# First layernorm of a two-layer attention and MLP kernel: x halves on two DMA queues, root on ScalarE, quarter copies, and Q of the first tiles in banks of its own

## Chip, cores, metric

The kernel runs on one core of one Trainium2 chip. The metric is device microseconds of one execution; lower is better. PE is TensorE, PEld its weight load, DVE VectorE, ACT ScalarE, POOL GpSimd, SP SyncE.

## The reference, cut to what matters

```python
x = A_x                                             # 2048 x 1024, bf16
x = x + A(_layernorm(x), A_wqkv, A_wo)              # sliding, dilated attention, 32 heads
x = x + B(_layernorm(x), B_w1, B_b1, B_w2, B_b2)    # MLP with GELU, 3584 wide
# ... the same two lines once more
# _layernorm: (x - mean) / sqrt(var + 1e-5) along the row, no scale, no shift
```

The change touches only the first layernorm (rows 0 to 511, "tiles" 0 to 3 of 128 rows) and the Q projection behind it.

## The kernel before

A row tile of x is loaded, its mean and variance are taken on VectorE, the inverse root on GpSimd; VectorE normalises, TensorE transposes 128x128 blocks into PSUM, ScalarE copies them to SBUF. Then the projections start. Tiles 0 and 1 go first, in 256-column matmuls over six chunks of Q; tiles 2 and 3 follow into the other half of the same PSUM banks.

```python
load_x(0, 0, 2)                              # x tiles 0 and 1 whole, SyncE's queue
load_wq_piece(wq_first[0], 0)                # Q weights in four pieces of 512 KB
load_x(0, 2, 4)
for k in range(2, KD, 2):
    load_wq_piece(wq_first[k // (KD // 2)], k)
# ...
def ln_stats(t, mv=None, rstd=None):         # ... bn_stats x2, bn_aggr on VectorE, then
    pool.tensor_tensor(out=rstd[:], in0=mv[:, 1:2], in1=eps_t[:], op=ALU.add)
    pool.tensor_tensor(out=rstd[:], in0=rstd[:], in1=mhalf[:], op=ALU.pow)
# ... in gen_qkv, for the first group of rows:
for kq in range(4 if n == 0 else 0):
    for c in range(6):
        first[c] = qkv_chunk(wq, c, xnT, first.get(c), kq * 2, (kq + 1) * 2, 0, 2)
        if (kq, c) in ((1, 5), (2, 5)):
            transpose_on_pe(*first_late.pop(0))        # tiles 2 and 3
for c in range(NCH):
    ps = qkv_chunk(wq, c, xnT, first[c], t0=2) if c in first else qkv_chunk(wq, c, xnT)
    act.copy(qT[:, c, :], ps[:])
```

A small helper keeps an engine's instructions in program order where it is switched on; elsewhere a scheduler orders them when the kernel is built.

## Time and profile before

| before | value |
|---|---|
| time, median of the six runs beside the changed kernel | 1232.80 us (1232.70 to 1232.99) |
| PE busy | 1226.2 of 1231.0 us |
| first projection matmul starts | 9.53 us |
| first copy of K starts | 26.39 us |
| end of the last addition to x, end of the span | 1228.40, 1230.96 us |

From the page of the kernel before, the busy times of the engines and the chain of work that ended last:

```profile
PE 1226.2 (100%) x5777; PEld 631.8 (51%) x5777; DVE 869.1 (71%) x886; ACT 304.1 (25%) x475; POOL 126.4 (10%) x238
...
PE 99%; DVE 0%; DMA 0%; ACT 0%; POOL 0%; issue 0%
```

PE is busy nearly all the time and makes up nearly the whole chain (99%). "Busy" alone would not say that PE is the limit, since its ends are modelled; the waits do. The view of waits of the kernel before, matmuls only (who waited for whom, us in total, times, longest us):

```profile
PE acc L118 <- DVE big L93: 1.1, 1, 1.1
PE acc L118 <- ACT xnT L93: 0.6, 1, 0.6
```

In 1231 us the view lists two waits of PE, both in the first 10 us (it leaves out idle time of 0.15 us or less). This is how the head runs; the timeline gives start, duration, engine, what is written and read, and in brackets how long the engine had been idle and what ended that:

```profile
0.80 1.28 ACT L93 ACT_TABLE_LOAD   x1 [0.80 <-PEq L592]
...
3.54 1.28 DVE L93 BATCH_NORM_STATS2 stats<-x 128x6 f32<-128x512 bf16 x2 [2.54 <-DMA x<-in_A_x_dram]
...
6.38 0.49 DVE L93 TENSOR_SCALAR xn<-x,mv,rstd 128x1024 bf16<-128x1024 bf16 x1
...
7.00 0.56 POOL L93 TENSOR_TENSOR rstd<-rstd,mhalf 128x1 f32<-128x1 f32 x1
...
7.59 0.55 DVE L93 TENSOR_SCALAR xn<-x,mv,rstd 128x1024 bf16<-128x1024 bf16 x1 [0.72 <-POOL rstd L93]
...
8.25 0.61 PE L211 MATMUL acc<-ident,xn 128*128 128x128 bf16 x8
...
8.89 1.07 ACT L93 COPY xnT<-acc 128x512 bf16<-128x512 bf16 x2 [0.24 <-PE acc L211]
...
9.53 2.78 PE L118 MATMUL acc<-xnT,wt 128*128 128x256 bf16 x24 [0.56 <-ACT xnT L93]
```

The activation table is loaded at 0.80 us, when ScalarE has nothing to do. Norm 0 (the normalising of tile 0) follows the statistics of tile 1 at once; norm 1 waits 0.72 us for GpSimd's power. ScalarE's half copy takes about 0.6 us and releases the first projection matmul at 9.53 us. The transposes of tiles 2 and 3 then stand between matmuls, and the view shows no wait for them. (The starts show a small one: tile 3's transposes begin at 14.00 us, 0.20 us after the matmul before instead of 0.11, when ScalarE's copy of tile 2 is done at 13.96.) The first copy of K is a good mark for the end of the head, as PE is unbroken behind it:

```profile
26.39 0.59 ACT L93 CAST kT<-acc 128x512 bf16<-128x512 f32 x1 [1.14 <-PE acc L118]
```

### The profile page before, as it was taken

Reading aid. Unit: us, or ns where it says so; the run is one execution under the profiler, and the core shown is the slowest. Engines: PE = TensorE matmul, PEld = TensorE weight load, DVE = VectorE, ACT = ScalarE, POOL = GpSimd, SP = SyncE. Lnnn points to the kernel's source line nnn. Section 1 sums busy time; section 2 is a strip of 40 time slices with the busy share of each in tenths; the row PEclk is TensorE's granted clock in tenths of the full one; section 3 lists DMA queues with packets and bytes.
Section 4 is the critical chain, followed back from the end, with each engine's and each line's share of the span. In section 5 each row is a group of like instructions: output and inputs, shape, how many; then the busy total and the mean of one; then the engine's idle time right before and its main releaser. Section 6 shows DMA issues by size and latency. Waiting matters only on the chain.

```text
span 1231.0 us, 13956 instructions
## 1 busy us (share of the span) xinstructions
PE 1226.2 (100%) x5777; PEld 631.8 (51%) x5777; DVE 869.1 (71%) x886; ACT 304.1 (25%) x475; POOL 126.4 (10%) x238
## 2 busy tenths in 40 slices
PE   9999999999999999999999999999999999999999
PEld 6666544456444564445544465444654444444444
DVE  7999899995996999376992779927599698012001
ACT  4333152014310143202431024310244101400310
POOL 4010011101021102200031000210000102000000
PEclk9999999999999999999999999999999999999999
DMA  9954568647487647756476565766556668446441
GB/s 307 283 180 140 184 198 202 207 138 235 144 197 227 178 163 180 220 171 187 148 189 222 171 171 169 175 220 197 171 183 158 185 200 204 160 159 196 154 135 53
DMA packets 219359, 226.63 MB, mean 184 GB/s; under 512 B 68562, under 2 KB 187488, under 8 KB 216224
## 3 DMA queue, kind: packets, MB, share of 16 engines
q1 hardware_dynamic: 214704, 208.69, 55.3%
q0 software_dynamic: 4592, 17.05, 6.0%
q8 instruction: 45, 0.74, 0.2%
q14 instruction: 18, 0.15, 0.1%
HBM read 197.40 MB, written 6.29 MB: 165 GB/s over the span
## 4 chain that ended last, share of the span: by engine, by line
PE 99%; DVE 0%; DMA 0%; ACT 0%; POOL 0%; issue 0%
PE acc L118 99%; DMA x<-in_A_x_dram 0%; DVE stats L93 0%; PE L L118 0%; PE acc L211 0%; PE L L211 0%; ACT xnT L93 0%; DVE mv L93 0%; DVE x L93 0%; POOL rstd L93 0%
## 5 line engine op out<-in xcount | busy, mean ns | idle before, releaser
L118 PE MATMUL acc<-xnT,wt 128*128 128x512 bf16 (+1 forms) x3376 | 720.8, 376 | 0.6 <-ACT xnT L93 0.6
L118 PEld LDWEIGHTS <-wt 128*128 128x128 bf16 x3376 | 399.1, 119 | 320.1 <-issue 1.6
L118 PE MATMUL acc<-wt,hT 128*128 128x512 bf16 (+1 forms) x1820 | 388.1, 376 | 0.0
L118 PEld LDWEIGHTS <-hT 128*128 128x128 bf16 x1820 | 178.1, 98 | 209.0
L93 DVE TENSOR_TENSOR big<-big 128x2048 bf16<-128x2048 bf16 (+2 forms) x184 | 245.5, 1359 | 2.9
L93 ACT ACTIVATE hT<-acc,b1T 128x512 bf16<-128x512 f32 x224 | 152.4, 688 | 331.1 <-PE acc L118 331.0
L93 DVE TENSOR_TENSOR big<-qT,kT 128x4096 bf16<-128x4096 bf16 x64 | 143.8, 2286 | 26.7 <-ACT kT L93 26.1
L93 DVE TENSOR_TENSOR big<-abc,vT 128x4096 bf16<-128x4096 bf16 x64 | 144.8, 2286 | 24.0 <-DMA abc<-a_d 23.5
L93 DVE TENSOR_TENSOR tmp<-acc,b2bc 128x512 f32<-128x512 f32 x56 | 38.6, 690 | 148.6 <-PE acc L118 145.1
L93 ACT CAST qT<-acc 128x512 bf16<-128x512 f32 x64 | 37.2, 586 | 341.7 <-PE acc L118 341.7
L118 PE MATMUL acc<-wt,oT 128*128 128x512 bf16 x448 | 97.8, 379 | 0.0
L93 DVE BATCH_NORM_STATS2 stats<-x 128x6 f32<-128x512 bf16 x128 | 83.4, 678 | 4.0 <-DMA x<-in_A_x_dram 3.4
L118 PEld LDWEIGHTS <-oT 128*128 128x128 bf16 x448 | 43.8, 98 | 52.8
L93 DVE TENSOR_TENSOR x<-acc,big 128x512 bf16<-128x512 f32 (+1 forms) x9 | 5.7, 633 | 90.0 <-PE acc L118 90.0
L93 POOL TENSOR_TENSOR rstd<-mv,eps_t 128x1 f32<-128x1 f32 x60 | 23.5, 391 | 434.2 <-DVE mv L93 434.2
L93 ACT CAST vT<-acc 128x512 bf16<-128x512 f32 x64 | 37.5, 586 | 83.1 <-PE acc L118 83.1
L93 ACT CAST kT<-acc 128x512 bf16<-128x512 f32 x64 | 37.4, 588 | 67.3 <-PE acc L118 67.3
L93 DVE TENSOR_TENSOR x<-acc,x 128x512 bf16<-128x512 f32 x64 | 42.5, 667 | 4.9 <-PE acc L118 4.7
L93 POOL TENSOR_TENSOR rstd<-rstd,mhalf 128x1 f32<-128x1 f32 x60 | 43.8, 730 | 4.7
L93 DVE TENSOR_SCALAR xn<-x,mv,rstd 128x1024 bf16<-128x1024 bf16 x52 | 28.2, 543 | 18.4 <-POOL rstd L93 18.4
L93 POOL DMA_DIRECT2D big<-big x24 | 13.5, 568 | 256.0 <-DVE big L93 239.1
L93 DVE TENSOR_TENSOR x<-tmp,x 128x512 bf16<-128x512 f32 x56 | 38.6, 690 | 1.6
(60 smaller groups left out, 251.1 us busy)
## 6 DMA issues: line engine op xcount, KB each, us to landing
wt<-in_B_w_dram SPq DMA_DIRECT2D x56, 1024.0 KB, 6.1
wt<-in_B_w_dram SPq DMA_DIRECT2D x64, 896.0 KB, 4.8
wt<-in_A_wqkv_dram SPq DMA_DIRECT2D x46, 1024.0 KB, 5.8
wt<-in_A_wo_dram SPq DMA_DIRECT2D x16, 1024.0 KB, 5.0
abc<-a_d POOLq DMA_DIRECT2D x32, 256.0 KB, 5.1
big<-big POOLq DMA_DIRECT2D x24, 256.0 KB, 7.8
x<-in_A_x_dram SPq DMA_DIRECT2D x16, 256.0 KB, 6.0
out_dram<-x SPq DMA_DIRECT2D x31, 128.0 KB, 2.2
```

The costliest lines, as they stand in the source:

```text
L93: inst = f(*args, **kwargs)
L118: return pe(nc.tensor.matmul(*args, **kwargs))
```

## The change

Its intent: start the projections earlier. x lands in halves over two queues, the root is spread over ScalarE and VectorE, copies come in quarters so that the first matmul needs only the first quarter, and Q of tiles 0 and 1 is copied out of banks of its own, so that two more chunks keep PE busy until tile 3 is there.

```diff
-    load_x(0, 0, 2)
+    for t in range(2):
+        sp.dma_start(x[t][:, 0:HALF], x_in[t * P:(t + 1) * P, 0:HALF])
+        act.dma_start(x[t][:, HALF:], x_in[t * P:(t + 1) * P, HALF:])
-    load_wq_piece(wq_first[0], 0)
-    load_x(0, 2, 4)
-    for k in range(2, KD, 2):
+    for k in range(0, KD, 2):
         load_wq_piece(wq_first[k // (KD // 2)], k)
+        if k < 4:
+            load_x(0, 2 + k // 2, 3 + k // 2)
 ...
+            act.activation(stds[tt][:], mvs[tt][:, 1:2], ACT.Sqrt, bias=eps_t[:])   # was two GpSimd ops
+            vec.reciprocal(rstd[:], stds[tt][:])
 ...
+        transpose_on_pe(xn0, xa[0][:, 0, :, :], parts=[act.copy] * 4)
+        transpose_on_pe(xn1, xa[0][:, 1, :, :], parts=[vec.tensor_copy] * 2 + [act.copy] * 2)
+        warm_up(2)
 ...
-                if (kq, c) in ((1, 5), (2, 5)):
+                if kq == 3:
+                    act.copy(qT[:, c, 0:2 * P], first[c][:, 0:2 * P])
+                if (kq, c) in ((2, 5), (3, 5)):
                     transpose_on_pe(*first_late.pop(0))
+        for c in range(6 if n == 0 else NCH, NCH):
+            ps = qkv_chunk(wq, c, xnT, t0=0, t1=2)
+            act.copy(qT[:, c, 0:2 * P], ps[:, 0:2 * P])
 ... (tiles 2 and 3 of all chunks then in fresh banks; a generator for later layernorms, same work)
```

More of the change, by code (lines that the diff above doesn't have):

```diff
@@ L181, in transpose_bias @@
         pe(nc.tensor.transpose(ps[:], b1_rows[:], ident[:KF, :KF]))
-        act.copy(b1T[:], ps[:])
+        return ps
     def ln_stats(t, mv=None, rstd=None):
@@ L205, in ln_norm, with transpose_on_pe @@
         return xn
-    def transpose_on_pe(xn, out, pst=None, halves=1):
+    def transpose_on_pe(xn, out, pst=None, parts=None):
         if pst is None:
@@ L211, in transpose_on_pe @@
             pe(nc.tensor.transpose(pst[:, k, :], xn[:, k * P:(k + 1) * P], ident[:]))
-        n = KD // halves
-        for h in range(halves):
-            act.copy(out[:, h * n:(h + 1) * n, :], pst[:, h * n:(h + 1) * n, :])
+        parts = parts or [act.copy]
+        n = KD // len(parts)
+        for h, copy in enumerate(parts):
+            copy(out[:, h * n:(h + 1) * n, :], pst[:, h * n:(h + 1) * n, :])
     last_transpose = [None]
@@ L227, in ln_first, with stats @@
         xa[0] = new_xnT()
-        vec.on = True
+        vec.on = act.on = True
         both = psum.tile([P, 2, KD, P], BF16, name="L", bufs=1)
-        stats = {}
-        def norm(tt):
-            xn = ln_norm(tt, *stats.pop(tt))
-            if tt < 2:
-                transpose_on_pe(xn, xa[0][:, tt, :, :], halves=2)
-            else:
-                first_late.append((xn, xa[0][:, tt, :, :], both[:, tt - 2, :, :]))
-            if tt == 0:
-                warm_up(4)
-        stats[0] = ln_stats(0)
-        stats[1] = ln_stats(1)
-        norm(0)
-        norm(1)
-        transpose_bias()
-        stats[2] = ln_stats(2)
-        stats[3] = ln_stats(3)
-        norm(2)
-        norm(3)
-        vec.on = False
+        mvs = {}
+        stds = {}
+        def stats(tt):
+            st6 = lnp.tile([P, 2, 6], F32, name="stats")
+            for h in range(2):
+                vec.bn_stats(st6[:, h, :], x[tt][:, h * HALF:(h + 1) * HALF])
+            mvs[tt] = lnp.tile([P, 2], F32, name="mv")
+            vec.bn_aggr(mvs[tt][:], st6[:])
+            stds[tt] = lnp.tile([P, 1], F32, name="std")
+            act.activation(stds[tt][:], mvs[tt][:, 1:2], ACT.Sqrt, bias=eps_t[:])
+        def norm(tt):
+            rstd = lnp.tile([P, 1], F32, name="rstd")
+            vec.reciprocal(rstd[:], stds[tt][:])
+            return ln_norm(tt, mvs[tt], rstd)
+        stats(0)
+        stats(1)
+        xn0 = norm(0)
+        xn1 = norm(1)
+        transpose_on_pe(xn0, xa[0][:, 0, :, :], parts=[act.copy] * 4)
+        ps = transpose_bias()
+        transpose_on_pe(xn1, xa[0][:, 1, :, :], parts=[vec.tensor_copy] * 2 + [act.copy] * 2)
+        warm_up(2)
+        act.copy(b1T[:], ps[:])
+        stats(2)
+        stats(3)
+        for tt in range(2, 4):
+            first_late.append((norm(tt), xa[0][:, tt, :, :], both[:, tt - 2, :, :]))
+        vec.on = act.on = False
+        act.hold()
     def new_xnT(pool=None):
@@ L273, in qkv_chunk @@
             mm(ps[:, t0 * P:t1 * P], lhsT=wts[k // (KD // 2)][:, k % (KD // 2), c::NCH], rhs=xnT[:, t0:t1, k, :],
-               start=(k == 0 and t0 == 0), stop=(k == KD - 1), skip_group_check=t1 - t0 < NTT)
+               start=(k == 0), stop=(k == KD - 1), skip_group_check=t1 - t0 < NTT)
         return ps
@@ L314, in gen_qkv @@
         if n == 0:
-            ln_early(1)
+            early_tiles = ln_early((1, None), (2, qk_next))
+            for _ in range(NTT):
+                next(early_tiles)
             wv = load_qkv(2)
-            ln_early(2, qk_next)
+            for _ in early_tiles:
+                pass
             load_x(3)
@@ L323, in gen_qkv @@
                 first[c] = qkv_chunk(wq, c, xnT, first.get(c), kq * (KD // 4), (kq + 1) * (KD // 4), 0, 2)
-                if (kq, c) in ((1, 5), (2, 5)):
+                if kq == 3:
+                    act.copy(qT[:, c, 0:2 * P], first[c][:, 0:2 * P])
+                if (kq, c) in ((2, 5), (3, 5)):
                     transpose_on_pe(*first_late.pop(0))
+        for c in range(6 if n == 0 else NCH, NCH):
+            ps = qkv_chunk(wq, c, xnT, t0=0, t1=2)
+            act.copy(qT[:, c, 0:2 * P], ps[:, 0:2 * P])
         for c in range(NCH):
-            ps = qkv_chunk(wq, c, xnT, first[c], t0=2) if c in first else qkv_chunk(wq, c, xnT)
-            act.copy(qT[:, c, :], ps[:])
+            t0 = 2 if n == 0 else 0
+            ps = qkv_chunk(wq, c, xnT, t0=t0)
+            act.copy(qT[:, c, t0 * P:], ps[:, t0 * P:])
             yield
@@ L504, in ln_a, with ln_early @@
             ln_tile((n % NG) * NTT + tt, tt, xa[n], ahead=ahead)
-    def ln_early(n, pool=None):
-        xa[n] = new_xnT(pool)
-        xns = bigp.tile([P, NTT, D], BF16, name="big") if pool is None else pool.tile([P, NTT, D], BF16, name="qT")
-        vec.on = True
-        s = [ln_stats(n * NTT)]
-        for tt in range(NTT):
-            if tt + 1 < NTT:
-                s.append(ln_stats(n * NTT + tt + 1))
-            ln_norm(n * NTT + tt, *s[tt], xns[:, tt, :])
-            sp.dma_start_transpose(xa[n][:, tt, :, :], xns[:, tt, :].rearrange("s (k p) -> s k p", p=P))
-        vec.on = False
+    def ln_early(*groups):
+        tiles = []
+        for n, pool in groups:
+            xa[n] = new_xnT(pool)
+            xns = bigp.tile([P, NTT, D], BF16, name="big") if pool is None else pool.tile([P, NTT, D], BF16, name="qT")
+            tiles += [(n * NTT + tt, xns[:, tt, :], xa[n][:, tt, :, :]) for tt in range(NTT)]
+        vec.on = True
+        ahead = ln_stats(tiles[0][0])
+        for i, (t, xn, xT) in enumerate(tiles):
+            mv_rstd = ahead
+            if i + 1 < len(tiles):
+                ahead = ln_stats(tiles[i + 1][0])
+            ln_norm(t, *mv_rstd, xn)
+            sp.dma_start_transpose(xT, xn.rearrange("s (k p) -> s k p", p=P))
+            if i + 1 == len(tiles):
+                vec.on = False
+            yield
     def stage(gen, count=None, sides=()):
@@ L542 @@
     pool.on = True
-    warm_up(16)
+    warm_up(14)
     ln_first()
```

## The prediction

> **What bounds the kernel.** TensorE. The page gives PE busy 1226.2 of 1231.0 us at full clock; the chain of waits is PE, unbroken from 9.5 us to 1228.0 us. The view of waits shows two for PE matmuls: 1.1 us for the warm-up's memset, 0.6 us for ScalarE's copy before the first projection matmul. So the change can only move that first matmul (9.53 us), or open a gap after it: a few us in 1233 at most.
>
> **The head before** (timeline, 0 to 22 us): x lands 3.51; statistics of tiles 0 and 1 end 6.46; norm 0 starts 6.38; norm 1 waits 0.72 us for GpSimd, ends 8.14; eight transposes 0.61; half copy 0.59; matmul 9.53.
>
> **What the change does there.**
> - x halves on two queues: the same 512 KB must come first; at most 0.2 us. The Trainium skill ("DMA: Bandwidth & Descriptors", Issuing engines are not separate DMA queues) says queues share engines and only issue time is saved; the two x issues took 0.87 us together here.
> - Square root on ScalarE, reciprocal on VectorE for two GpSimd operations (0.38 + 0.56). But in the built order the activation-table load stands behind the wait for tile 0's aggregate, where before it ran at 0.80 us. A load costs 1.28 us in this trace, and the one at 154.7 us did wait for VectorE first. So: aggregate seen at about 4.9, load until 6.2, both roots until 6.8, norm 0 starts about 6.8 (0.4 later), norm 1 about 7.45, ending about 8.0 (0.15 earlier). The load eats most of the gain.
> - Quarter copies, tile 1's first two on VectorE: about 0.3 to 0.37 each (from 1.01 for 1024 columns, 0.59 for 512) instead of 0.59. The two new warm-up matmuls end about 9.1. First projection matmul about 9.1: gain 0.4 us.
>
> **What it gives back.**
> - Q of the first group becomes 128 matmuls of 256 columns at 0.109 us, before 96 of them and 16 of 512 at 0.216: +0.05 us.
> - In ScalarE's order six Q copies (about 0.3 each) stand between the copies of tiles 2 and 3 (1.0 each). Tile 3's ends about 17.3 us; PE wants it about 17.0: a new wait of 0 to 0.7 us, 0.3 expected.
> - One more table load before the first exponential (67 us) delays VectorE about 1 us. VectorE's attention products end 2.2 us before the output projection starts (125.3), so PE should not feel it.
>
> **Prediction:** 1232.6 us, range 1231.6 to 1233.6; faster by over 2% 0.01, within 2% 0.98, slower 0.01.
>
> **What the profile would show.** Right: table load from about 4.9 us; norm 0 near 6.8, norm 1 ending near 8.0; first projection matmul near 9.1; a PE wait for tile 3's copy at about 17 us; first K copy within 0.3 us of 26.39; no other PE wait. Wrong: first projection matmul before 8.6 or after 9.6; no wait at 17 us (gain 0.4) or one over 0.8 (a loss); a PE wait at 60 to 130 us.
>
> **What would make it wrong.** The table load hidden after all (gain near 1 us); ScalarE's queue starting late, second halves of x landing after 3.9 us; VectorE copies from PSUM over 0.5 us each, which also pushes tiles 2 and 3 back; weight pieces late behind the reordered x loads.

## The result

The changed kernel takes 1233.43 us (median of six runs, 1233.09 to 1233.62), the kernel before 1232.80 in the same rounds. The ratio is 1.0005, with a 95% interval of 0.9992 to 1.0018. A ratio here is the mean time of one kernel's runs over that of the other's of the same rounds, so it is not quite the ratio of the medians. Every one of the six runs is above every one of the six before, and the trace says where 0.6 to 0.8 us went.

Waits of PE and of its weight loads in the changed kernel, first 40 us:

```profile
PE acc L118 <- DVE big L93: 1.1, 1, 1.1
...
PE acc L213 <- DVE xn L93: 0.8, 1, 0.8
...
PEld L118 <- DMA wt<-in_A_wqkv_dram: 0.2, 1, 0.2
PE acc L118 <- ACT xnT L93: 0.2, 1, 0.2
```

The 0.8 us before the transposes is no loss in itself (two warm-up matmuls fewer stand there). The last two lines are new and lie behind the first projection matmul. The head, as the timeline shows it:

```profile
3.61 1.29 DVE L93 BATCH_NORM_STATS2 stats<-x 128x6 f32<-128x512 bf16 x2 [2.61 <-DMA x<-in_A_x_dram]
...
4.93 0.21 DVE L93 BATCH_NORM_AGGREGATE mv<-stats 128x2 f32<-128x12 f32 x1
...
5.22 1.28 ACT L93 ACT_TABLE_LOAD   x1 [5.22 <-DVE mv L93]
...
6.51 0.48 ACT L93 ACTIVATE std<-mv,eps_t 128x1 f32<-128x1 f32 x2
6.84 0.16 DVE L93 RECIPROCAL rstd<-std 128x1 f32<-128x1 f32 x1 [0.31 <-ACT std L93]
7.04 0.55 DVE L93 TENSOR_SCALAR xn<-x,mv,rstd 128x1024 bf16<-128x1024 bf16 x1
...
7.70 0.55 DVE L93 TENSOR_SCALAR xn<-x,mv,rstd 128x1024 bf16<-128x1024 bf16 x1
...
8.31 0.62 PE L213 MATMUL acc<-ident,xn 128*128 128x128 bf16 x8
...
8.97 0.49 DVE L93 COPY xnT<-acc 128x256 bf16<-128x256 bf16 x2 [0.73 <-PE acc L213]
...
9.41 4.34 PE L118 MATMUL acc<-xnT,wt 128*128 128x256 bf16 x36
...
12.22 1.30 PEld L118 LDWEIGHTS <-wt 128*128 128x128 bf16 x12 [0.23 <-DMA wt<-in_A_wqkv_dram]
```

The table load now starts at 5.22 us, released by VectorE's aggregate of tile 0 (the step that joins the statistics of its two halves), and both square roots stand behind it. VectorE's reciprocal waits 0.31 us for ScalarE. Norm 0 is 0.66 us later than before (7.04 against 6.38), norm 1 0.11 us later (7.70 against 7.59). The quarter copies then win 0.20 us: from the end of tile 1's transposes to the first projection matmul 0.47 us (8.94 to 9.41) against 0.67 (8.86 to 9.53). Tile 1's transposes end 0.08 us later, so the net gain at that matmul is 0.12 us. At 12.22 us a weight load waits for the third piece of Q weights.

The chain of waits of the changed kernel from tile 2's transposes on (start, us, what):

```profile
13.76 0.46 PE L L213 x8
...
14.24 1.01 ACT xnT L93
15.25 1.66 ACT qT L93 x6
16.91 0.93 ACT xnT L93
...
17.88 22.26 PE acc L118 x134
```

Here ScalarE has the chain for 3.6 us: tile 2's copy, six copies of Q, tile 3's copy. PE has matmuls of its own for nearly as long, and waits for the rest. The PE starts nearest to it are 17.45 and 17.88 us: 0.43 us apart where 0.11 is usual, so 0.32 us are lost. The view of waits says 0.2, because it counts from the modelled end of the last matmul.

The first copy of K:

```profile
26.79 0.58 ACT L93 CAST kT<-acc 128x512 bf16<-128x512 f32 x1 [1.35 <-PE acc L118]
```

It is 0.40 us later than before: -0.12 + 0.22 (weight piece: the two starts there are 0.27 and 0.17 us apart instead of 0.11) + 0.32 = 0.42. (The rest, about 0.02 us less, is explained under experiment 5.) This offset stays to the end, where the last addition to x ends 0.41 us later (1228.81 against 1228.40). But the span is 0.78 us longer: 0.37 us more arise after the last addition, 2.93 us in place of 2.56. No part of the change runs there.

The trace's SyncE waits for DMA semaphores after the last addition, start in us and the semaphore's number (left out are the issue of the last output DMA and one wait for semaphores outside this list, which comes ahead of it; the last output DMA is number 116 before, 100 in the changed kernel):

```
before:   1228.88 wait 101   1228.94 wait 111   1229.01 wait 112   1229.07 wait 113   1229.13 wait 114
          1229.24 wait 115   1230.00 wait 116   1230.06 wait 117   1230.12 drain ... span ends 1230.96
changed:  1230.41 wait 100   1230.47 wait 102   1230.54 wait 112   1230.60 wait 113   1230.66 wait 114
          1230.72 wait 115   1230.78 wait 116   1230.84 wait 118   1230.90 drain ... span ends 1231.74
```

A semaphore here is a counter that a DMA raises as it lands. SyncE waits for eight semaphores of its DMAs one after the other, 0.06 us each. Before, the DMA that lands last (1229.98 us) is the seventh of the eight. In the changed kernel it (1230.39 us) is the first, and seven waits that are long fulfilled follow it. The last DMA itself is no later: it lands 1.58 us after the end of the last addition in both. The built program gives its DMAs these semaphores in turn, and the changed kernel has two DMAs more, which moves the last one from the seventh place to the first. Six more waits of 0.06 us behind it are the 0.37 us. That is only a reading of one pair of traces; experiments 1, 2 and 6 test it.

### The profile page after: what moved, and what is told of

It is laid out like the page before. It is cut to its first block, busy times and chain, and to the rows that moved or that the text cites. A ratio compares the mean times of both kernels' runs of the same rounds, so it can differ in the third digit from the quotient of the medians.

```text
span 1231.7 us, 13998 instructions
## 1 busy us (share of the span) xinstructions
PE 1226.3 (100%) x5789; PEld 632.5 (51%) x5789; DVE 870.1 (71%) x892; ACT 306.4 (25%) x490; POOL 122.7 (10%) x230
## 4 chain that ended last, share of the span: by engine, by line
PE 99%; ACT 0%; DMA 0%; DVE 0%; issue 0%; ACTq 0%
PE acc L118 99%; DMA x<-in_A_x_dram 0%; ACT xnT L93 0%; ACT qT L93 0%; DVE stats L93 0%; ACT L93 0%; PE acc L213 0%; PE L L118 0%; DVE xn L93 0%; PE L L213 0%; DVE x L93 0%; ACT std L93 0%; DVE mv L93 0%; DVE rstd L93 0%; PE acc L183 0%
## 5 line engine op out<-in xcount | busy, mean ns | idle before, releaser
L93 ACT CAST qT<-acc 128x512 bf16<-128x512 f32 (+1 forms) x72 | 38.0, 545 | 341.2 <-PE acc L118 341.2
L93 DVE TENSOR_REDUCE z<-e 128x128 f32<-128x1024 f32 x8 | 15.3, 1918 | 33.7 <-ACT e L93 33.7
```

What stands on the lines that cost most here:

```text
L93: inst = f(*args, **kwargs)
```

## The experiments

Twelve runs, all with correct outputs, in three batches; the kernels of a batch share one chip and its runs of the kernel before (medians 1232.88, 1232.94 and 1232.70 us): runs 1 to 4, 5 to 8 and 9 to 12. Positions are those of one profiled execution per kernel, so small differences between batches may be the chip's. Every verdict was "same" at 2%; what follows rests on positions in the traces, and times stand beside them. Where no profile line is shown, positions and landing times of single DMAs are read from the trace.

| run | median us (runs) | before | first projection | first K copy | after the last addition |
|---|---|---|---|---|---|
| before | 1232.80 (6) | | 9.53 | 26.39 | 2.56 |
| changed | 1233.43 (6) | 1232.80 | 9.41 | 26.79 | 2.93 |
| 1 before, x1 on ACT's queue | 1233.61 (4) | 1232.88 | 10.83 | 27.60 | 2.55 |
| 2 changed, one queue | 1233.20 (4) | 1232.88 | 8.93 | 26.55 | 2.93 |
| 3 changed, early table | 1232.96 (4) | 1232.88 | 8.80 | 25.96 | 2.93 |
| 4 changed, tile 3 on DVE | 1234.24 (4) | 1232.88 | 9.26 | 27.47 | 2.92 |
| 5 changed, copy order | 1232.77 (5) | 1232.94 | 9.40 | 26.25 | 2.92 |
| 6 before, two DMAs more | 1233.06 (5) | 1232.94 | 9.53 | 26.30 | 2.93 |
| 7 combination | 1232.36 (5) | 1232.94 | 9.27 | 26.11 | 2.50 |
| 8 combination, load order | 1232.59 (5) | 1232.94 | 9.16 | 26.08 | 2.49 |
| 9 whole tiles | 1233.82 (5) | 1232.70 | 8.78 | 27.40 | 2.50 |
| 10 halves | 1233.75 (5) | 1232.70 | 8.65 | 27.61 | 2.49 |
| 11 changed, root on GpSimd | 1233.19 (5) | 1232.70 | 9.44 | 26.60 | 2.94 |
| 12 changed again | 1233.22 (5) | 1232.70 | 9.46 | 26.62 | 2.92 |

### 1. Before, tile 1 of x through ScalarE's queue

```diff
-    load_x(0, 0, 2)
+    load_x(0, 0, 1)
+    act.dma_start(x[1][:], x_in[P:2 * P, :])
```

> The kernel before, with one edit: x tile 1 is loaded through ScalarE's DMA queue. In the changed kernel 0.40 us of the 0.74 us longer span arise in the first 26 us (first K copy 26.79 against 26.39) and 0.34 us after the last addition to x (from its end to the end of the span 2.94 us against 2.56). Theory A: the end of the program takes longer because a second DMA queue is in use; then this kernel's stretch after the last addition is about 2.9 us, its first K copy stays within 0.1 us of 26.39, and it is about 0.3 us slower than before. Rival B: the 0.34 us at the end is scatter from run to run; then 2.5 to 2.6 us and no slower than before.

Theory A (a second queue costs the end) fell: a second queue is in use and the end takes 2.55 us. The expectation that the head stays was wrong too, and this is the more useful miss. Statistics of tile 0 in the head of this run:

```profile
4.84 1.29 DVE L93 BATCH_NORM_STATS2 stats<-x 128x6 f32<-128x512 bf16 x2 [3.85 <-DMA x<-in_A_x_dram]
```

Tile 0 landed at 4.82 us and tile 1 at 4.65, where the kernel before has 3.51 and 4.14 on one queue. The two transfers share the engines, so the tile that is needed first comes 1.3 us later. The first projection matmul slips to 10.83 us and the first K copy to 27.60.

### 2. The changed kernel on one queue

```diff
-        act.dma_start(x[t][:, HALF:], x_in[t * P:(t + 1) * P, HALF:])
+        sp.dma_start(x[t][:, HALF:], x_in[t * P:(t + 1) * P, HALF:])
```

> The changed kernel with all four x halves on SyncE's queue, so no second queue. Theory A: the stretch after the last addition falls to about 2.6 us and the kernel gains 0.3 us against the changed one. Rival B: no change at the end. In the head: the last half of x is issued about 0.9 us later (each issue takes 0.43 us), so if the second queue's saved issue time matters, the first projection matmul comes later than 9.41 by up to 0.5 us; if the loads of weights are bound by what the DMA engines move, the first K copy stays within 0.15 us of 26.79.

The end stays at 2.93 us without a second queue: theory A falls a second time. Rival B (scatter) falls as well, as every kernel with two DMAs more than before shows 2.92 to 2.94. The head moved the other way than feared. The halves of tile 0 landed at 3.10 and 3.41 us (3.58 and 3.76 on two queues), those of tile 1 at 4.65 and 4.93 (4.09 and 4.32):

```profile
3.13 1.29 DVE L93 BATCH_NORM_STATS2 stats<-x 128x6 f32<-128x512 bf16 x2 [2.13 <-DMA x<-in_A_x_dram]
...
8.93 2.81 PE L118 MATMUL acc<-xnT,wt 128*128 128x256 bf16 x24
...
11.99 1.53 PE L118 MATMUL acc<-xnT,wt 128*128 128x256 bf16 x12 [0.24 <-DMA wt<-in_A_wqkv_dram]
```

Statistics start 0.48 us sooner and so does the first projection matmul. Then 0.46 us of PE time go in waiting for the third weight piece at 11.99 us, and the first K copy gains only 0.24 us. The other profiles with tile 0 in halves agree: its later half lands at 3.41 to 3.50 us on one queue (four profiles) and at 3.59 to 3.83 on two (six). Against experiment 4, which has the changed kernel's head on the same chip, the first projection matmul is 0.33 us sooner (8.93 against 9.26). The second queue is no gain in this head; one queue in the order of need was better.

### 3. The table load early

```diff
     pool.memset(eps_t[:], EPS)
+    root0 = const.tile([P, 1], F32, name="root0")
+    act.activation(root0[:], eps_t[:], ACT.Sqrt)
```

> The changed kernel plus one early square root of a constant on ScalarE, so that the activation-table load runs at about 1 us instead of behind tile 0's aggregate at 5.22 us. Theory C: the load (1.28 us) costs about 0.5 us at the first projection matmul (8.9 instead of 9.41), but this is not kept: the third weight piece lands at 12.18 us and x of tile 3 at 10.91 us whatever ScalarE does, so the PE wait for the weight piece grows from 0.2 to about 0.7 us and the first K copy stays within 0.1 us of 26.79. Rival D: the load is the whole loss; then the first K copy comes at about 26.3 us and the kernel is about 0.5 us faster than the changed one.

```profile
1.73 1.28 ACT L93 ACT_TABLE_LOAD   x1 [1.73 <-PEq L623]
...
6.29 0.11 DVE L93 RECIPROCAL rstd<-std 128x1 f32<-128x1 f32 x1
...
6.43 0.55 DVE L93 TENSOR_SCALAR xn<-x,mv,rstd 128x1024 bf16<-128x1024 bf16 x1
...
7.09 0.55 DVE L93 TENSOR_SCALAR xn<-x,mv,rstd 128x1024 bf16<-128x1024 bf16 x1
...
8.80 4.12 PE L118 MATMUL acc<-xnT,wt 128*128 128x256 bf16 x36
```

The reciprocal no longer waits for ScalarE, and the first projection matmul comes at 8.80 us, 0.61 us sooner. Of this 0.17 us are an earlier landing of x (statistics at 3.44 against 3.61), so about 0.44 us are the table load. Experiment 4 is a closer control: the changed kernel's head on the same chip, with statistics from 3.46 us and the late table load, has its first projection matmul at 9.26 us, which again leaves 0.44. Theory C expected the gain to be lost again at the third weight piece; it was not, as that piece landed at 11.25 us in this run and not at 12.18. The first K copy at 25.96 us beats rival D's 26.3. The landing of weights differs between profiles of programs with the same loads, and C had taken one landing time for a constant. The time, 1232.96 us, is near that of the kernel before because the end still costs 0.37 us and tile 3 still waits.

### 4. Tile 3's copy on VectorE

```diff
-                    transpose_on_pe(*first_late.pop(0))
+                    transpose_on_pe(*first_late.pop(0), parts=[vec.tensor_copy] if kq == 3 else None)
```

> The changed kernel with tile 3's transposed copy (1024 columns) on VectorE instead of ScalarE, where it stood behind six Q copies. Theory: the PE gap before 17.88 us (about 0.3 us) goes; first K copy at about 26.48 us, span 0.3 us shorter than the changed kernel's. Rival: something else holds PE there (a later arrival of tile 3's norm or of a bank), and the gap stays over 0.2 us.

The opposite came out:

```profile
14.99 0.61 PE L213 MATMUL L<-ident,xn 128*128 128x128 bf16 x8
...
16.57 1.28 DVE L93 BATCH_NORM_STATS2 stats<-x 128x6 f32<-128x512 bf16 x2
...
17.77 0.67 DVE L93 COPY xnT<-L 128x1024 bf16<-128x1024 bf16 x1
...
18.50 1.75 PE L118 MATMUL acc<-xnT,wt 128*128 128x256 bf16 x14 [1.14 <-DVE xnT L93]
```

The transposes were done at 15.6 us and the copy itself takes 0.67 us instead of 1.0, but the scheduler put it behind the statistics of a later tile, so it started at 17.77. The PE starts around it are 17.08 and 18.50 us, a loss of 1.3 us. This experiment does not show that the place in ScalarE's queue was the cause of the first gap, only that the place in VectorE's queue decides this one.

### 5. Tile 3's copy further ahead in ScalarE's queue

```diff
-                if kq == 3:
+                if kq == 3 and c < 2:
                     act.copy(qT[:, c, 0:2 * P], first[c][:, 0:2 * P])
                 if (kq, c) in ((2, 5), (3, 5)):
                     transpose_on_pe(*first_late.pop(0))
+        for c in range(2, 6 if n == 0 else 0):
+            act.copy(qT[:, c, 0:2 * P], first[c][:, 0:2 * P])
```

The built order has four Q copies before tile 3's copy instead of six.

> The changed kernel with ScalarE's copy of tile 3 moved ahead of the last Q copies (only four of the six now stand before it). Theory: the wait before tile 3's first matmul comes from the place of that copy in ScalarE's queue (in the run with the copy on VectorE it stood behind statistics there and the gap grew to 1.4 us), so here the gap of 0.43 us between two PE starts at about 17.5 us goes to 0.11, and the first K copy comes 0.32 us sooner for the same start: 17.06 us after the first projection matmul plus any wait for weights, against 17.38 in the changed kernel. Rival: a bank or the norm of tile 3 holds PE; then the gap stays over 0.3 us. Weight pieces: their landing scattered by 1.7 us between runs of one and the same head (third piece 12.18 and 10.65 us), so a wait for them may or may not show.

```profile
PE acc L213 <- DVE xn L93: 1.8, 1, 1.8
PE acc L118 <- DVE big L93: 1.0, 1, 1.0
```

These are all of PE's waits that the view lists for this run, both of them before the first projection matmul. From that (9.40 us) to the first K copy are 26.25 - 9.40 = 16.84 us (taken before rounding). (The expectation says 17.06; it subtracted only the wait for tile 3 from a distance that also held a wait for weights of 0.22 us.) That is close to the 16.86 us of the kernel before, but not because 128 narrow matmuls in place of 96 narrow and 16 wide are free. The profile before holds the 0.09 us wait of tile 3's transposes; two other runs of the old order without that wait (experiments 1 and 6) have 16.76 and 16.77 us. Against these the changed order costs about 0.08 us, near the predicted 0.05, and in the first pair of profiles the two small terms cancel. The gap before tile 3 is gone, so the 0.32 us were the place of that copy in ScalarE's queue.

### 6. Before, two late DMAs more

```diff
-            load_x(3)
+            load_x(3, 0, 2)
+            for t in range(S // P - 2, S // P):
+                for h in range(2):
+                    sp.dma_start(x[t][:, h * HALF:(h + 1) * HALF], ...)
```

> The kernel before with two of the late x loads split in halves: two more DMAs, one queue, nothing else. At the end of the program SyncE waits for eight DMA semaphores one after the other, 0.06 us each; in the kernel before the DMA that lands last is waited for near the end of that list, in the changed one second, and six waits follow it. DMAs take these semaphores in turn, and the changed kernel has two DMAs more. Theory: the place of the last DMA in the list is what costs the 0.37 us; then this kernel has 2.93 us after the last addition instead of 2.56, its first K copy stays at about 26.4 us, and it is about 0.35 us slower than before. Rival: the second queue or the changed head costs it; then 2.56 us.

The theory held: 2.93 us after the last addition, with one queue and the old head. (The expectation says "second" and "six waits" because it counted the wait for another queue that comes ahead; among the eight it is the first, with seven behind it.) SyncE's list is as in the changed kernel:

```
1230.01 wait 101 (last output DMA, landed 1229.99)   1230.07 wait 111   ... six more, 0.06 us each ...   1230.51 drain
```

The size of the loss in time is less sure: 1233.06 against 1232.94 us, 0.12 us of the 0.35 expected, inside the scatter of both (1232.96 to 1233.48, and 1232.57 to 1233.36).

### 7 and 8. Combinations

Run 7 is the changed kernel with tile 0 of x in halves and tile 1 whole on SyncE's queue, the early root of experiment 3 and the order of experiment 5. It has one DMA more than the kernel before, so the last one should take the eighth place and no wait should follow it. Run 8 adds:

```diff
-        if k < 4:
-            load_x(0, 2 + k // 2, 3 + k // 2)
+        if k in (2, 4):
+            load_x(0, 1 + k // 2, 2 + k // 2)
 ...
-        stats(2)
-        stats(3)
         for tt in range(2, 4):
+            stats(tt)
             first_late.append(...)
```

> The changed kernel with x of tile 0 in halves and tile 1 whole, all on SyncE's queue; the early table load; and tile 3's copy ahead of the last Q copies. Three DMAs fewer than two more: one more than before, so the last DMA should be waited for last: about 2.5 us after the last addition. x of tile 0 lands in halves at about 3.1 and 3.4 us as in the run with all halves on SyncE's queue; norm 0 starts at about 6.1 us, first projection matmul at about 8.5 us, first K copy at 25.6 us plus waits for weight pieces of 0 to 1 us in sum. About 1.0 us faster than the kernel before if weights arrive in time, 0.2 if not.

> As the combined kernel, with the second weight piece ahead of x of tile 2 and the third ahead of x of tile 3, and norm 2 before the statistics of tile 3. If the combined kernel is held by weight pieces, this one removes that wait: first K copy at 25.6 us, about 1.0 us faster than before and up to 0.7 faster than the combined one. If it isn't held, both are the same within 0.1 us.

The end came out as expected: 2.50 us, the last DMA is the last one waited for (1229.76 us, then the drain). The head did not. Tile 1 of x, loaded whole behind two halves, landed at 5.28 and 5.18 us, not before 4.2, so the first projection matmul came at 9.27 and 9.16 us instead of 8.5. From there to the first K copy neither kernel shows a PE wait of over 0.1 us, for weights, tile 3 or anything else, so the two are alike to 0.03 us at the first K copy, as expected for "not held". Run 7 is the best kernel: its five runs (1231.82 to 1232.55 us) are all below the nine of the kernel before in that batch (1232.57 to 1233.36), 0.58 us between the medians. Its ratio, 0.9994 with 0.9981 to 1.0008, does not exclude 1, so that it is the faster one is likely from the separate runs, but this test cannot confirm it. With the changed kernel it shares no batch.

### 9 and 10. Two attempts at more

Run 9 is run 8 with tiles 0 and 1 of x whole, and one late x load in halves for the DMA count. Run 10 has both in halves on SyncE's queue and seven late x pieces more.

```diff
-    for h in range(2):                       # run 8: tile 0 in halves, then load_x(0, 1, 2)
+    load_x(0, 0, 2)                          # run 9; run 10: the loop of experiment 2
 ...
-            load_x(3)
+            for t, m in zip(range(S // P - 4, S // P), (1, 1, 1, 2)):      # run 10: (3, 3, 3, 2)
+                for h in range(m):
+                    sp.dma_start(x[t][:, cols], ...)                       # pieces of columns
```

> A version meant to beat both: the changed kernel with x of tiles 0 and 1 whole on SyncE's queue as before (in the two runs with tile 0 in halves and tile 1 whole, tile 1 landed at 5.2 us, in the kernel before at 4.14), the early table load, weight pieces two and three ahead of x of tiles 2 and 3, norm 2 before the statistics of tile 3, tile 3's copy ahead of the last Q copies, and one late x load in halves, so that there is one DMA more than before and the last one is waited for last. Expected: norm 0 at 6.45 us, norm 1 ends at 7.6, first projection matmul at 8.9, no wait until the first K copy at 25.75 us (8.9 + 16.84), 2.50 us after the last addition: span 1230.3 us, about 0.7 us faster than before. If x of tile 1 lands after 4.8 us again, the first projection matmul is later by as much.

> The same with both x tiles in halves on SyncE's queue (landed at 3.10, 3.41, 4.65 and 4.93 us in the run that did this) and seven late x pieces more, for the same place of the last DMA. Expected: norm 0 at 6.3 us, first projection matmul at 8.65, first K copy at 25.5 us, span 1230.0 us: halves are worth 0.25 us on one queue. If they are worth nothing, equal to the whole-tile version within 0.1 us.

The first projection matmuls came as expected (8.78 and 8.65 us), and both kernels lost: every run of both (lowest 1233.47 and 1233.21 us) is above the nine of the kernel before (highest 1233.07), and run 10's ratio, 1.0015 with 1.0003 to 1.0028, excludes 1. The end is as planned: run 10 has exactly eight DMAs more than run 9, so its last one takes the same place, and both end 2.49 to 2.50 us after the last addition. The view of waits of run 9, PE only:

```profile
PE L L213 <- ACT xnT L93: 0.9, 1, 0.9
PE acc L118 <- DMA wt<-in_A_wqkv_dram: 0.8, 2, 0.6
```

PE now ran ahead of its weights (third piece at 11.76 us, wanted at 11.4). And the edit "norm 2 before the statistics of tile 3" backfired: x of tile 3 landed at 12.43 us in run 9, its square root stands in ScalarE's order before tile 2's copy, and so that copy waited for tile 3's statistics:

```profile
13.20 0.62 PE L213 MATMUL L<-ident,xn 128*128 128x128 bf16 x8
...
14.68 0.30 ACT L93 ACTIVATE std<-mv,eps_t 128x1 f32<-128x1 f32 x1 [2.31 <-DVE mv L93]
...
15.24 1.00 ACT L93 COPY xnT<-L 128x1024 bf16<-128x1024 bf16 x1
...
16.29 0.61 PE L213 MATMUL L<-ident,xn 128*128 128x128 bf16 x8 [0.92 <-ACT xnT L93]
```

Tile 2's transposes end at 13.8 us; its copy starts at 15.24. In run 8 the same order did no harm, because there x of tile 3 landed at 10.56 us. Run 10 has the same two losses, and in its profile, which is of the slowest of its five runs (1237.05 us, median 1233.75), two later waits of matmuls for weights (1.1 us before 54.6 and 1.6 us before 57.3 us), where its extra x pieces stand ahead of weights in SyncE's queue. That the pieces are the cause of the late waits was not tested apart.

### 11 and 12. The root back on GpSimd; the changed kernel again

```diff
-            act.activation(stds[tt][:], mvs[tt][:, 1:2], ACT.Sqrt, bias=eps_t[:])
-            vec.reciprocal(rstd[:], stds[tt][:])
+            pool.tensor_tensor(out=stds[tt][:], in0=mvs[tt][:, 1:2], in1=eps_t[:], op=ALU.add)
+            pool.tensor_tensor(out=stds[tt][:], in0=stds[tt][:], in1=mhalf[:], op=ALU.pow)
```

Run 12 has no edit.

> The changed kernel with its inverse root back on GpSimd (add and power, 0.4 and 0.56 us), all else kept. If the late table load eats the gain of the root, this costs nothing: norm 0 starts at about 6.5 us for x landing at 3.6, norm 1 ends at 8.2 (8.25 in the changed kernel), first projection matmul within 0.1 us of 9.41. If root and reciprocal are worth something although the load is late, the first projection matmul comes 0.3 us or more later.

> The changed kernel once more, beside the others on one chip. 2.93 us after the last addition as before. The gap before tile 3's first matmul stays at 0.43 us between starts. The wait for the third weight piece (landed 12.18 us) is expected to go or to stay with the scatter of the landings, as it is not in the program: first K copy 26.5 to 26.8 us.

With the root on GpSimd the first projection matmul is at 9.44 us, without the edit at 9.46 and 9.41, and the times are 1233.19 and 1233.22 us (runs 11 and 12). The root's way over ScalarE and VectorE, with its table load behind the aggregate, is worth nothing. In run 12 the third weight piece landed at 11.34 us and no wait for it shows; the gap before tile 3 is 0.43 us and the end 2.92 us, as before. So 0.32 and 0.37 us belong to the program, and the 0.22 us of the first profile do not; whether they came with that execution or with its chip is not shown. The loss repeats: run 12's five runs (1233.14 to 1233.51 us) are all above the nine of the kernel before in this batch (1232.42 to 1233.07), 0.52 us between the medians.

## Why the prediction was right or wrong

The measured 1233.43 us lie in the predicted range and "within 2%" was right. The opening claim, that only the start of the first projection matmul and gaps behind it count, held for PE and not for the span. The centre, 1232.6 us, had the wrong sign: the change was taken for a gain of 0.2 us and lost about 0.6. That the range still covers it, by 0.17 us, is partly luck: the largest part of the loss came from a place that the prediction did not look at, and a range of 1 us to each side was wide enough for it. The sum by its terms, in us against the kernel before:

| term | predicted | changed, first profile | changed, run 12 |
|---|---|---|---|
| first projection matmul | -0.43 | -0.12 | -0.07 |
| narrow matmuls (+0.08), less the 0.09 us wait that only the profile before has | +0.05 | about 0 | about 0 |
| wait for tile 3's copy | +0.3 | +0.32 | +0.32 |
| wait for the third weight piece | named as a risk | +0.22 | 0 |
| end of the program | not in the sum | +0.37 | +0.36 |
| span | -0.1 | +0.78 | +0.60 |

- "The activation-table load stands behind the wait for tile 0's aggregate": right, and the main point of the head. It ran from 5.22 us (predicted 4.9). The Trainium skill ("ScalarE: Activation LUTs", What ACT_TABLE_LOAD costs) gives 1283 ns for the load, as measured here. It adds a drain of about 1380 ns to every switch; no run here shows one, before the load or after it. The roots start 1.29 us after the start of the load (5.22 to 6.51), and before, a load directly behind another activation costs 1.30 us from its start to the next activation (171.61 to 172.91), and 1.32 us from the end of the activation before it (171.59). The trace's number is used.
- "Norm 0 near 6.8, norm 1 ending near 8.0": mis-sized. Measured 7.04 and 8.25. The aggregate ended at 5.14 us and not at 4.9, since the halves brought x no sooner, and the reciprocal (0.16 us) with its hand-over came on top of tile 0's root (6.51 to about 6.8 us).
- "x halves on two queues: at most 0.2 us": right in size, and it was no gain at all; one queue in halves did better (experiment 2). Experiment 1 agrees with the Trainium skill ("DMA: Bandwidth & Descriptors", Issuing engines are not separate DMA queues): transfers from two queues run on the same engines and interleave, here to the cost of 1.3 us for the tile needed first.
- "Quarter copies about 0.3 to 0.37": close. VectorE's took 0.28 to 0.29 us, ScalarE's 0.37 to 0.41. The trace has the end of VectorE's first quarter at 9.26 us, and the first projection matmul 0.15 us later.
- "A new wait of 0 to 0.7 us, 0.3 expected" for tile 3's copy "about 17.3 us": right, 0.32 us at 17.88, and shown to come from the six Q copies ahead of it (experiment 5).
- "First K copy within 0.3 us of 26.39": missed in the first profile (0.40), met in run 12 (0.23). The difference is the third weight piece, which the prediction named as what could go wrong.
- "PE should not feel" the second table load: right. The offset against the kernel before is 0.40 us at 61 us, 0.40 at the start of the output projection (125.71 against 125.31) and 0.41 at 1228 us. VectorE's attention products did come 1.35 us later and ended 1.25 us ahead of it.
- Not in the prediction at all: the end of the program. "The change can only move that first matmul, or open a gap after it" is the step that failed. It left out that the last 2.56 us, after the last addition to x, are the landing of the last output DMA and a fixed list of SyncE's waits, in which that DMA's place depends on the number of DMAs in the whole program. These 0.37 us are the largest single term.

What stays open: why weights land up to 1.7 us apart between profiles with the same loads (first piece 6.57 to 8.31 us, third 10.65 to 12.18), and why a whole tile of x behind two halves lands at 5.18 to 5.28 us and behind a whole tile at 4.14 to 4.75 (experiments 7 and 8 against the kernel before, 6 and 9); 0.47 us of it is its later issue. For the weights, much of the spread lies between the batches: on one chip the first piece lands at 6.57 and 6.69 us (experiments 4 and 3), on another at 7.37 and 7.47 (11 and 12), so chip and chance were not separated.

## What to carry to other kernels

Before counting a square root as a cheap replacement, look in the built order for the activation-table load and for what it waits for; an early dummy activation of the same set moved it into idle time and was worth 0.44 us at the first projection matmul (one profile, with a control on the same chip), where the root alone was worth nothing. In this kernel, which one engine fills, the place of a copy in its engine's queue mattered more than its length: tile 3's copy cost 0.32 us behind six small copies and 1.3 us on an engine that copies faster, behind the statistics of a later tile. When differences of some tenths of a microsecond are weighed, compare positions in the trace (first matmul, first copy of a stage, last addition) as well as the total, since here about half of the total came from the order of waits at the end.

## What the Trainium skill lacked or had wrong

- "ScalarE: Activation LUTs" (What ACT_TABLE_LOAD costs): the drain of about 1380 ns per switch does not show. Load and next activation are 1.29 to 1.30 us apart, load included; from the end of the activation before it to the start of the next are 1.32 us.
- The same page (Step-by-step, Table-load gate) says that the load is placed right before the activation. It lacks that the load may then carry that activation's wait for another engine, as the one at 5.22 us did, and that an early activation of the same set moves it (to 1.73 us in experiment 3).
- "DMA: Bandwidth & Descriptors" (Issuing engines are not separate DMA queues): right that transfers interleave, but it gives saved issue time as the only effect. It lacks the cost: with two 256 KB tiles on two queues the first landed at 4.82 us instead of 3.51.
- "Runtime: NRT & Kernel Launch" (The ~15µs preamble/postamble breakdown) lists a barrier after the kernel, but no page tells of SyncE's waits for DMA semaphores before it: they come in a fixed order, 0.06 us each, so the place of the last DMA among the eight decides whether 2.49 to 2.56 us (seventh or eighth) or 2.92 to 2.94 us (first) pass after the last addition to x.
- No page has how far landings in a program's head differ between profiles: the third 512 KB weight piece landed between 10.65 and 12.18 us in five profiles with the same loads (the changed kernel twice, experiments 4, 5 and 11), over several chips.
